# Loading 112 rows of keys instead of 128, and taking a norm's root one part later in VectorE's order, in a fused attention and feed-forward kernel

## The chip, the cores and the metric

The kernel runs on one core of one Trainium2 chip. The metric is the device time of one execution in microseconds, as the median of several runs. TensorE (PE in the profile) does the matmuls, VectorE (DVE) and GpSimd (POOL) elementwise work, ScalarE (ACT) activations and copies, and SyncE (SP) issues nearly all DMA transfers.

## The reference

Eight batches of 576 tokens, eight heads of 64 columns: a linear attention without softmax, a root-mean-square norm per token and head, and a feed-forward layer with an exact gelu over all 4608 tokens (512 to 2048 to 512), all in float32.

```python
def _attn_ref(q, k, v, g_norm):
    kv = np.einsum('bhsd,bhse->bhde', k, v)
    out = np.einsum('bhsd,bhde->bhse', q, kv)
    rms = np.sqrt(np.mean(out * out, axis=-1, keepdims=True) + 1e-06)
    return (out / rms * g_norm).astype(np.float32)

def _moe_ref(x, w_in, w_out):
    h = x @ w_in
    g = 0.5 * h * (1.0 + erf(h * np.float32(1.0 / np.sqrt(2.0))))
    return (g @ w_out).astype(np.float32)
```

## The kernel before

The 4608 tokens are cut into nine chunks of 512. Every instruction's place is set by the order in which the code is written, engine by engine; there is no scheduler that reorders.

**Keys and values.** For each batch `b` and pair of heads `p`, the sum of keys times values (`sum_kv`, matmuls on line 175) needs 576 rows: four blocks of 112 rows side by side in one tile (`kv_main`, 4 KB per row) and a tail of 128 rows. In memory the 112 rows of `kv_main` are padded with zeros to 128. `load_kv` (the transfer on line 130) brings all 128 rows, and the matmuls use the first `KROWS` = 112. The sums lie in a bank of PSUM called `a0` or `a1`, and `place_kv` copies them out (line 186 on ScalarE, line 188 twice on VectorE). All four pairs of batch 0 and of batch 1 are loaded at the start, eight of the 32 loads, among the activations `qT` and the weights, all on SP's one queue.

**The start.** Twelve warm-up matmuls (line 782) run on TensorE while the first loads land. Then come, for chunk 0: the key sums of batch 0, pair by pair, the projections (line 229), the squares (ScalarE), the root (VectorE, lines 299 to 305), and in between the key sums of pairs 0 and 1 of batch 1. Line 894 expands the root over the heads on TensorE, lines 885 and 900 multiply it in on VectorE, and line 660 is the first matmul of the feed-forward layer. Weights are split into high and low halves on ScalarE and VectorE as they arrive.

**Chunks 2 to 8** use sums and differences of blocks of the weights, seven products where eight would be. Layer 1 is a row of parts: `first_part(j)` is 24 matmuls, `second_part(j)` 18 (line 559), for j from 0 to 7, in the order first 0, first 1, second 0, first 2, second 1, first 3, second 2, first 4, second 3 and so on. Part j uses one of three pairs of PSUM banks, chosen by `j % 3`, so first part 5 takes the banks acc2 and acc3 of part 2 again. What frees those banks are the two gelus of second part 2 (line 591, ScalarE), and ahead of each gelu stand sums on VectorE (line 550):

```python
    def second_part(at, j, blocks):
        ...
        add(a[:, right], a[:, right], u[:, right])
        product(at, j, 6, b[:, right])
        add(v[:, left], b[:, right], u[:, left])
        add(b, b, v)
```

While chunk c runs, the next chunk's norm is prepared between the parts (`within_layer1`). For chunk 2 (`FAST`), the squares are summed after first part 3 (`fold`), the key sums of pairs 0 and 1 of batch 4 follow on TensorE, and then the root: `rsqrt` issues nine small VectorE instructions (lines 296 to 314), `place_kv` one copy on ScalarE and two on VectorE. The root is spread by VectorE (line 327) and multiplied in by GpSimd (line 323) from second part 2 on (`SCALES`). In `within_layer1` a place is written `(j, second)`: `(3, False)` is behind first part 3, `(2, True)` behind second part 2, which comes next.

Of the kernel before, what the change touches and what calls it, by code (L numbers as in the profile page):

```python
# [19 lines left out]
KROWS = 112  # L20
# [3 lines left out]
FAST = 2  # L24
# [13 lines left out]
def linear_attn_rms_gelu_ffn(  # L38
# [16 lines left out]
    nc = tc.nc  # L55
# [19 lines left out]
    def bank(name):  # L75
        return psum.tile([P, 512], F32, name=name)
# [27 lines left out]
    def block_tile(name, dtype):  # L104
        return const.tile([P, 2 * DM + EXTRA.get(name, 0)], dtype, name=name)
# [7 lines left out]
    def late_tile(name):  # L113

        if name not in late:
            late[name] = block_tile(name, I32)[:, :2 * DM].bitcast(F32)
        return late[name]

    def load_kv(b, p):

        early = b == 0 or (b == 1 and p > 1)
        if early:
            main = late_tile(f"w_out{NF - 1 - p if b == 0 else NF - 3 - p}")
        elif b == 2 and p > 1:
            main = block_tile(f"s{p - 1}", F32)
        elif b > 2 and b != FAST + 2 and p > 1:
            names["keys", p], main = take(stays=True)
        else:
            main = work.tile([P, 2 * DM], I32, name="kv_main", bufs=2).bitcast(F32)
        nc.sync.dma_start(out=main, in_=kv_main[b, p])  # L130
        main = main.rearrange("p (a n) -> p a n", a=2)[:KROWS]
        if b == 0:
            tails = late_tile(f"w_in{NF - 1}")[:TAIL].rearrange("p (a n) -> p a n", a=NP)
            if p == 0:
                nc.sync.dma_start(out=tails, in_=kv_tail[0])
            tail = tails[:, p]
        else:
            at = slice((p - 2) * 2 * P, (p - 1) * 2 * P)
            if early:
                tail = late_tile(f"w_in{NF - 5}")[:, at]  # L140
            elif b == 2 and p > 1:
                if p == 2:
                    kv_ps["tails"] = block_tile("s0", F32)
                tail = kv_ps["tails"][:, at]
            elif b > 2 and b != FAST + 2 and p > 1:
                if p == 2:
                    names["keys", 0], kv_ps["tails"] = take(stays=True)
                tail = kv_ps["tails"][:, at]
            else:
                tail = work.tile([P, 2 * P], I32, name="kv_tail", bufs=2).bitcast(F32)  # L150
            tail = tail[:TAIL]
            nc.sync.dma_start(out=tail, in_=kv_tail[b, :, p])
        tail = tail.rearrange("p (a n) -> p a n", a=2)
        parts = [main[:, :, j * P:(j + 1) * P] for j in range(NJ)] + [tail]
        kv_in[b, p] = [(t[:, 0], t[:, 1]) for t in parts]
# [6 lines left out]
    def rows(r):  # L162
        return slice(r * D, (r + 1) * D)

    def sum_kv(b, pairs, ps=None, first=0):

        if ps is None:
            first = pairs[0]
            ps = kv_ps[b, first] = next_bank("a")
        for p in pairs:  # L170
            n = p - first
            for j, (k, v) in enumerate(kv_in.pop((b, p))):

                for r in (slice(0, D), slice(D, 2 * D)):
                    nc.tensor.matmul(  # L175
                        out=ps[r, n * D:(n + 1) * D], lhsT=k[:, r], rhs=v[:, r],
                        start=(j == 0), stop=(j == NJ),
                    )

    def place_kv(b, pairs):  # L180

        ps = kv_ps.pop((b, pairs[0]))
        ps = ps[:, :len(pairs) * D].rearrange("p (n d) -> p n d", d=D)
        at = slice(pairs[0], pairs[-1] + 1)
        t = kv[b % 2]
        nc.scalar.copy(out=t[:, at, 0], in_=ps)
        for r in range(2):
            nc.vector.tensor_copy(out=t[rows(r), at, 1], in_=ps[rows(1 - r)])
# [346 lines left out]
    def take(dtype=F32, stays=False, first=()):  # L535
        name = next(n for n in [*(n for n in first if n in free), *free]
                    if not (stays and n in RINGS))
        free.remove(name)
        return name, block_tile(name, dtype)[:, :2 * DM]
# [211 lines left out]
    g_row = late_tile(f"w_in{NF - 6}")[:1, P:2 * P]  # L751
    ones, eps = (late_tile(f"w_in{NF - 6}")[:1, a * P:(a + 1) * P] for a in (2, 3))
    load_kv(0, 0)
    first.load(0)
    load_kv(0, 1)
    first.load(1)
    for p in (2, 3):
        load_kv(0, p)
# [34 lines left out]
    for d in range(0, 2 * D, BLK):  # L793
        h = d // D * D
        nc.gpsimd.tensor_tensor(
            out=fold[:, d:d + BLK], in0=ident[:, h:h + BLK], in1=ident[:, h + BLK:h + 2 * BLK],
# [24 lines left out]
    def column(n, t):  # L821
        return n_fold + 2 * ((n - 2) * NG + t)

    def sum_squares(n):
# [12 lines left out]
        out=half_g, in0=ps[:, :1], scalar1=0.5, scalar2=None, op0=ALU.mult  # L837
# [3 lines left out]
        out=sums[:, :P], lhsT=ones, rhs=eps, start=True, stop=False,  # L841
# [4 lines left out]
        out=root_g, in0=half_g, scalar1=D ** 0.5, scalar2=None, op0=ALU.mult  # L846
# [9 lines left out]
    for half in range(2):  # L856
# [6 lines left out]
        out=sums[:, :n_fold].rearrange("p (g b) -> p g b", g=2), lhsT=fold,  # L863
# [3 lines left out]
    for half in range(2):  # L867
        nc.scalar.activation(
            out=first.block((1, half)),
            in_=first.ps.pop((1, half)).rearrange("p (a n) -> p a n", a=2), func=AF.Copy,  # L870
# [11 lines left out]
    for half in range(2):  # L882
# [3 lines left out]
            out=first.o_all[:, half], in0=first.ps.pop((0, half)), scalar=root_g, in1=bc,  # L886
# [4 lines left out]
        for t in range(NG):  # L891
            for h in range(2):
                at = column(n, t) + h
                nc.tensor.matmul(
                    out=bc[rows(h), t * P:(t + 1) * P],
# [210 lines left out]
    for s in range(PLAIN * NF):  # L1106
        c, i = divmod(s, NF)
# [182 lines left out]
    def scale_next(c, at):  # L1290

        nxt = attn[c + 1]
        for n, (when, block) in enumerate(SCALES[c]):
            if when == at:
                if n % 2 == 0:
                    names["spread"], spreads[:] = zip(*(take() for _ in range(2)))
                nxt.scale(block, nc.gpsimd, spreads[n % 2][:, :CH])
                if n % 2:
                    free.extend(names.pop("spread"))
        for k in ADDS[c].get(at, ()):  # L1300
            nxt.add_blocks(k, nc.gpsimd)

    def within_layer1(c, j, second):

        at = j, second
        if c + 1 < NCH:
            nxt = attn[c + 1]
            if c == FAST and j == 0:
                if second:
                    nxt.project(1, [bank(f"a{half}") for half in range(2)])  # L1310
                for half in range(2):
                    nxt.squares((int(second), half))
            if c == FAST and at == (3, False):
                sums[c] = nxt.fold(bank("a0"))
                kv_ps[c + 2, 0] = bank("a1")
                sum_kv(c + 2, (0, 1), kv_ps[c + 2, 0])
            if at == ((3, False) if c == FAST else (0, False)):
                nxt.inv = nxt.rsqrt(sums.pop(c))
                if c + 2 < B:
                    place_kv(c + 2, (0, 1) if c == FAST else range(NP))  # L1320
            scale_next(c, at)
        if c == FAST and second and j in (2, 3):
            load_kv(c + 2, j)
        if c == FAST + 1 and at == (0, True):
            attn[c + 2].load(1)
# [49 lines left out]
    for c in range(FAST, NCH):  # L1375
        at = attn[c]
# [3 lines left out]
        for j, second in parts_of_layer1():  # L1380
# [16 lines left out]
            if j < NJ2 - 1:  # L1397
                within_layer1(c, j, second)
# [73 lines left out]
```

## Time and profile before

| | |
|---|---|
| median of three runs | 775.45 us (775.06 to 775.83) |
| profiled execution | 776.38 us, of which its span (first to last instruction) 774.6 us |
| TensorE matmuls | 768.6 us busy, 99% of the span |
| VectorE | 582.7 us, 75% |
| ScalarE | 358.4 us, 46% |
| GpSimd | 180.5 us, 23% |
| DMA queue of SP | 243.83 MB, 87.4% of 16 engines |
| granted TensorE clock | 1.0 throughout |

In the rows of a timeline the columns are the start and the duration in us, the engine (PEld is TensorE's weight load, SPq the issue of a transfer), the line, the operation, the tiles and their shape; brackets hold the idle time ahead of it and what ended that. In a list of waits they are the engine and line, what was waited for, the total in us, how often, and the longest. In a row by window stand the window, the busy times of PE, PEld, DVE, ACT and POOL, the clock, the DMA share and GB/s.

### The profile page before, as it was taken

To read this page: it belongs to the slowest core of one execution; us is meant where nothing else is said; L and a number is where in the kernel's file an instruction comes from. 1 tells how busy PE (TensorE), PEld (TensorE's weight loads), DVE (VectorE), ACT (ScalarE), POOL (GpSimd) and SP (SyncE) were. 2 spreads that over 40 slices of the span, in tenths; PEclk is the share of its full clock that TensorE was granted. 3 is DMA by queue.
4 is the path that set the end of the run, shared out by engine and by line. 5 is a ranking of instruction groups with operands and counts; after the bars stand their busy time and mean duration, and the time that the engine had idled before them with its cause. 6 is when DMAs were issued, how large, how long until landed. Compare 5 with 4: busy or idle time off the path is not lost.

```text
span 774.6 us, 16805 instructions
## 1 busy us (share of the span) xinstructions
PE 768.6 (99%) x6604; PEld 727.1 (94%) x6604; DVE 582.7 (75%) x1043; ACT 358.4 (46%) x689; POOL 180.5 (23%) x155
## 2 busy tenths in 40 slices
PE   8999999999999999999999999999999999999998
PEld 7888888888899999999999999999999999999998
DVE  3999867989878994679577857686778776955784
ACT  3777635533464571347135633454245524632460
POOL 1000025433736200620054004500450045001200
PEclk9999999999999999999999999999999999999999
DMA  9999953869999999979998899879996899799974
GB/s 345 407 409 357 369 191 132 290 231 337 331 370 370 318 340 347 365 268 327 403 336 296 320 402 333 317 222 336 380 336 215 299 355 337 245 316 346 333 246 167
DMA packets 90177, 244.89 MB, mean 316 GB/s; under 512 B 8948, under 2 KB 31988, under 8 KB 90100
## 3 DMA queue, kind: packets, MB, share of 16 engines
q1 hardware_dynamic: 90096, 243.83, 87.4%
q8 instruction: 52, 0.85, 0.4%
q14 instruction: 25, 0.20, 0.1%
q10 hardware_dynamic: 4, 0.00, 0.0%
HBM read 207.09 MB, written 34.08 MB: 311 GB/s over the span
## 4 chain that ended last, share of the span: by engine, by line
PE 94%; DMA 2%; DVE 2%; ACT 1%; issue 0%; SPq 0%; ACTq 0%
PE acc L1233 24%; PE acc L559 20%; PE h L559 12%; PE acc L693 11%; PE h L670 11%; PE h L1233 6%; PE a L1233 5%; PE a L175 2%; DMA kv_main<-kv_main 1%; PE a L229 1%; PE h L660 1%; DMA w_in<-qT 1%; PE acc L229 1%; DVE w_out L1017 0%; PE a L281 0%
## 5 line engine op out<-in xcount | busy, mean ns | idle before, releaser
L693 PE MATMUL acc<-w_out,gh 128*128 128x512 f32 x256 | 79.3, 391 | 0.0
L670 PE MATMUL h<-x,w_in 128*128 128x512 f32 x264 | 70.5, 391 | 0.0
L559 PE MATMUL acc<-w_in,w_in 128*128 128x256 f32 x510 | 66.3, 277 | 0.6 <-ACT x L591 0.6
L1233 PE MATMUL acc<-w_in,w_in 128*128 128x256 f32 x528 | 65.0, 276 | 0.0
L559 PE MATMUL acc<-x,w_in 128*128 128x256 f32 x480 | 64.0, 276 | 0.0
L559 PEld LDWEIGHTS acc<-w_in,w_in 128*128 128x128 f32 x510 | 61.7, 188 | 1.3 <-ACT x L591 0.8
L1233 PEld LDWEIGHTS acc<-w_in,w_in 128*128 128x128 f32 x528 | 62.2, 188 | 0.0
L670 PEld LDWEIGHTS h<-x,w_in 128*128 128x128 f32 x264 | 49.2, 188 | 10.7 <-ACT w_in L646 0.3
L559 PEld LDWEIGHTS acc<-x,w_in 128*128 128x128 f32 x480 | 58.9, 188 | 0.0
L693 PEld LDWEIGHTS acc<-w_out,gh 128*128 128x128 f32 x256 | 47.7, 188 | 10.1 <-issue 0.2
L693 PE MATMUL acc<-w_out,gl 128*128 128x512 f32 x128 | 49.8, 389 | 0.0
L550 DVE TENSOR_TENSOR gl<-acc,gh 128x256 f32<-128x256 f32 (+1 forms) x77 | 34.2, 444 | 20.3 <-ACT gh L572 16.4
L679 ACT ACTIVATE gh<-h 128x512 fp32r<-128x512 f32 x32 | 19.1, 598 | 60.5 <-PE h L670 60.5
L559 PE MATMUL h<-w_in,w_in 128*128 128x256 f32 x306 | 40.1, 278 | 0.0
L559 PE MATMUL h<-x,w_in 128*128 128x256 f32 x288 | 39.0, 278 | 0.0
L572 ACT COPY gh<-h 128x256 f32<-128x256 f32 x21 | 7.8, 372 | 67.3 <-PE h L559 67.3
L1233 PE MATMUL acc<-w_in,w_out 128*128 128x256 f32 x306 | 38.9, 276 | 0.0
L323 POOL TENSOR_TENSOR o<-o,w_in 128x512 f32<-128x512 f32 x10 | 13.0, 1298 | 107.9 <-ACT s L591 54.2
L550 DVE TENSOR_TENSOR gl<-h,gh 128x256 f32<-128x256 f32 x42 | 17.6, 419 | 26.2 <-ACT gh L572 23.5
L559 PEld LDWEIGHTS h<-w_in,w_in 128*128 128x128 f32 x306 | 37.2, 188 | 0.1
L1233 PEld LDWEIGHTS acc<-w_in,w_out 128*128 128x128 f32 x306 | 36.6, 188 | 0.0
L559 PEld LDWEIGHTS h<-x,w_in 128*128 128x128 f32 x288 | 35.5, 188 | 0.0
(374 smaller groups left out, 1906.3 us busy)
## 6 DMA issues: line engine op xcount, KB each, us to landing
w_in<-products_in SPq DMA_DIRECT2D x168, 512.0 KB, 5.5
w_in<-products_out SPq DMA_DIRECT2D x133, 512.0 KB, 5.0
products_in<-w_in SPq DMA_DIRECT2D x36, 256.0 KB, 5.4
w_in<-w_in SPq DMA_DIRECT2D x16, 512.0 KB, 10.2
kv_main<-kv_main SPq DMA_DIRECT2D x16, 512.0 KB, 5.7
w_out<-w_out SPq DMA_DIRECT2D x16, 512.0 KB, 10.2
q<-qT SPq DMA_DIRECT2D x15, 512.0 KB, 6.7
products_out<-w_out SPq DMA_DIRECT2D x16, 256.0 KB, 6.4
```

The source lines that it names most:

```text
L175: nc.tensor.matmul(out=ps[r, n * D:(n + 1) * D], lhsT=k[:, r], rhs=v[:, r], start=(j == 0), stop=(j == NJ),)
L229: nc.tensor.matmul(out=ps[rows(h), p % 2 * HALF + a:p % 2 * HALF + e], lhsT=kv[b % 2][rows(half), p, h ^ half], rhs=q[rows(half), h, a:e], ...
L323: eng.tensor_tensor(out=o, in0=o, in1=bc, op=ALU.mult)
L550: return eng.tensor_tensor(out=out, in0=x, in1=y, op=op)
L559: nc.tensor.matmul(out=out, lhsT=y, rhs=x[:, z, kb], start=first and kb + i == 0, stop=kb == 1 and i == 2, skip_group_check=True,)
L572: nc.scalar.copy(out=u[:, left], in_=a[:, left])
L660: nc.tensor.matmul(out=h[:, half * HALF:(half + 1) * HALF], lhsT=ws[i].bitcast(F32)[:, p * P:(p + 1) * P], rhs=at.block((p // 2, half))[:, ...
L670: nc.tensor.matmul(out=h, lhsT=parts["in", i][:, w][:, p * P:(p + 1) * P], rhs=at.x[p][:, x], start=(m + p == 0), stop=(m == 2 and p == NP ...
L679: nc.scalar.activation(out=gh, in_=h, func=AF.Gelu)
L693: nc.tensor.matmul(out=ps, lhsT=x[:, ts], rhs=parts["out", i][:, w], start=(i == 0 and m == 0), stop=(m == 2 and (i == NF - 1 or (i, t) == ...
L1233: nc.tensor.matmul(out=self.bank[name][a][:, a * HALF:(a + 1) * HALF], lhsT=x[:, at], rhs=y, start=(k in (0, 2, 1) and n + p + m == 0 and ...
```

## The change

Both edits are one line each. The load takes the first 112 rows, in the tile and in memory. In chunk 2 the root and the copies of the key sums are issued behind second part 2 instead of ahead of it; `fold` and the key sums themselves stay where they are.

```diff
@@ -127,7 +127,7 @@
             names["keys", p], main = take(stays=True)
         else:
             main = work.tile([P, 2 * DM], I32, name="kv_main", bufs=2).bitcast(F32)
-        nc.sync.dma_start(out=main, in_=kv_main[b, p])
+        nc.sync.dma_start(out=main[:KROWS], in_=kv_main[b, p, :KROWS])
         main = main.rearrange("p (a n) -> p a n", a=2)[:KROWS]
         if b == 0:
             tails = late_tile(f"w_in{NF - 1}")[:TAIL].rearrange("p (a n) -> p a n", a=NP)
@@ -1314,7 +1314,7 @@
                 sums[c] = nxt.fold(bank("a0"))
                 kv_ps[c + 2, 0] = bank("a1")
                 sum_kv(c + 2, (0, 1), kv_ps[c + 2, 0])
-            if at == ((3, False) if c == FAST else (0, False)):
+            if at == ((2, True) if c == FAST else (0, False)):
                 nxt.inv = nxt.rsqrt(sums.pop(c))
                 if c + 2 < B:
                     place_kv(c + 2, (0, 1) if c == FAST else range(NP))
```

VectorE's order in chunk 2 before, from the last sum of first part 3 on (m, y and t are the root's, a_2658 the key sums, acc_2553 and acc_2554 the banks of part 2):

```order
L550 TENSOR_TENSOR gh<-h_2624,gh 128x256
L296 TENSOR_SCALAR m<-a_2656 128x64
L299 TENSOR_SCALAR y<-m 128x64
L305 SCALAR_TENSOR_TENSOR t<-y 128x64
L310 TENSOR_TENSOR t<-t,m 128x64
L305 SCALAR_TENSOR_TENSOR t<-t 128x64
L305 SCALAR_TENSOR_TENSOR y<-t,y 128x64
L305 SCALAR_TENSOR_TENSOR t<-y 128x64
L314 TENSOR_TENSOR t<-t,m 128x64
L305 SCALAR_TENSOR_TENSOR y<-t,y 128x64
L188 COPY kv_68<-a_2658 64x2x64 x2
L550 TENSOR_TENSOR acc_2553<-acc_2553,gh 128x256
```

The same place after:

```order
L550 TENSOR_TENSOR gh<-h_2624,gh 128x256
L550 TENSOR_TENSOR acc_2553<-acc_2553,gh 128x256
L550 TENSOR_TENSOR gl<-acc_2554,gh 128x256
L550 TENSOR_TENSOR acc_2554<-acc_2554,gl 128x512
L296 TENSOR_SCALAR m<-a_2656 128x64
L299 TENSOR_SCALAR y<-m 128x64
L305 SCALAR_TENSOR_TENSOR t<-y 128x64
L310 TENSOR_TENSOR t<-t,m 128x64
L305 SCALAR_TENSOR_TENSOR t<-t 128x64
```

The three sums of second part 2 now stand ahead of the root's nine instructions and the two copies instead of behind them; the spread of the root (L327) follows next in both.

ScalarE's order there before, from the copy of first part 3's first product on:

```order
L572 COPY gh<-h_2623 128x256
L186 COPY kv_68<-a_2658 128x2x64
L591 ACTIVATE x_2716<-acc_2553 128x2x256
L591 ACTIVATE w_in_2717<-acc_2554 128x2x256
L572 COPY gh<-acc_2728 128x256
```

And after:

```order
L572 COPY gh<-h_2623 128x256
L591 ACTIVATE x_2701<-acc_2553 128x2x256
L591 ACTIVATE w_in_2702<-acc_2554 128x2x256
L186 COPY kv_68<-a_2658 128x2x64
L572 COPY gh<-acc_2728 128x256
```

The copy of the key sums goes behind the two gelus of part 2. TensorE's order is unchanged, and on SP only the shape of the key loads differs. The first of them, after:

```order
L130 DMA w_out_118<-kv_main 112x1024
L135 DMA w_in_120<-kv_tail 128x1024
L203 DMA w_in_122<-qT 128x512
L130 DMA w_out_124<-kv_main 112x1024
L203 DMA w_in_122<-qT 128x512
L130 DMA w_out_127<-kv_main 112x1024
L130 DMA w_out_129<-kv_main 112x1024
L203 DMA w_in_131<-qT 128x512 x2
L611 DMA w_in_136<-w_in 128x1024
L130 DMA kv_main<-kv_main 112x1024
L152 DMA kv_tail<-kv_tail 128x256
L130 DMA kv_main<-kv_main 112x1024
```

Every row of `kv_main` read 128x1024 before; no transfer has moved past another.

## The prediction

> **What bounds the kernel now.** I read the page first (busy time by engine, the chain that ended last), then what TensorE's matmuls (PE) waited for, then the timeline round the two places that the change touches.
>
> ```profile
> PE 768.6 (99%) x6604; PEld 727.1 (94%) x6604; DVE 582.7 (75%) x1043; ACT 358.4 (46%) x689; POOL 180.5 (23%) x155
> ...
> q1 hardware_dynamic: 90096, 243.83, 87.4%
> ...
> PE 94%; DMA 2%; DVE 2%; ACT 1%; issue 0%; SPq 0%; ACTq 0%
> ```
>
> ```profile
> PE acc L559 <- ACT x L591: 0.6, 1, 0.6
> ...
> PE a L175 <- DMA kv_main<-kv_main: 0.4, 1, 0.4
> ```
>
> PE is busy for 768.6 of 774.6 us. The chain is PE's for 94%, so an edit pays only where PE stands still or is held back. From 29 us to the end the list of PE's waits holds a single entry, 0.6 us for a gelu (L591) in chunk 2; before that, one wait for a load of keys, 0.4 us. The change touches just these two. The DMA engines are at 87% in the mean, but PE waits for no transfer after that one, so the key loads after the start, however long, are put at nothing: their cover is that they are issued several parts ahead. The profiled execution took 776.38 us, 0.93 us above the median of the runs (775.45). I subtract the same microseconds from both.
>
> **Part 1, the root in chunk 2.** The timeline of that place, by engine rather than by time:
>
> ```profile
> 230.58 0.84 PE L559 MATMUL acc<-x,w_out 128*128 128x256 f32 x6
> ...
> 233.98 0.84 PE L559 MATMUL h<-w_in,w_in 128*128 128x256 f32 x6
> ...
> 236.76 3.67 PE L559 MATMUL acc<-w_in,w_in 128*128 128x256 f32 x30 [0.58 <-ACT x L591]
> ...
> 241.63 2.88 PE L559 MATMUL h<-w_in,w_in 128*128 128x256 f32 x24
> ...
> 232.08 0.41 DVE L550 TENSOR_TENSOR gh<-h,gh 128x256 f32<-128x256 f32 x1
> 232.41 0.21 DVE L296 TENSOR_SCALAR m<-a 128x64 f32<-128x64 f32 x1
> ...
> 234.91 0.23 DVE L305 SCALAR_TENSOR_TENSOR y<-t,y 128x64 f32<-128x64 f32 x1
> 235.15 0.59 DVE L188 COPY kv<-a 64x128 f32<-64x128 f32 x2
> 235.66 0.41 DVE L550 TENSOR_TENSOR acc<-acc,gh 128x256 f32<-128x256 f32 x1
> ...
> 236.57 0.70 DVE L550 TENSOR_TENSOR acc<-acc,gl 128x512 f32<-128x512 f32 x1
> 237.18 0.70 DVE L327 STREAM_TRANSPOSE s<-y 128x512 f32<-128x512 f32 x1
> 238.20 0.42 DVE L550 TENSOR_TENSOR gl<-acc,gh 128x256 f32<-128x256 f32 x1 [0.32 <-ACT gh L572]
> ...
> 236.11 0.60 ACT L591 ACTIVATE x<-acc 128x512 f32<-128x512 f32 x1 [5.37 <-DVE acc L550]
> ```
>
> The six matmuls at 230.58 are the last of second part 2, so both its banks are complete at 231.42. VectorE (DVE) gets to their sums only at 235.66: from 232.41 it runs the root's nine instructions and the two copies of a key sum, 235.66 - 232.41 = 3.25 us. The gelu that frees bank acc2 starts at 236.11, and PE, which is to put first part 5 into that bank, stands until 236.76.
>
> What PE loses: a first part is 24 matmuls, a second part 18. Second part 3 starts at 233.98; it (18), first part 5 (24) and second part 4 (18) follow, then first part 6 at 241.63. Second part 4 ends where first part 6 begins, so 60 matmuls took 7.65 us. The undisturbed pace comes from two rows, 24 matmuls in 2.88 us and 6 in 0.84: (2.88 - 0.84) / 18 = 0.1133 each, so 60 take 6.80. The loss is 0.85 us, of which the named wait is 0.58, the rest the refill round it. I take 0.85, since both ends of that count are starts of matmuls in the trace.
>
> What takes its place: with the sums first, the three run from 232.41 for the 1.52 us that they take now (235.66 to 237.18), to 233.93. The first gelu follows 0.45 us behind the first sum (as 236.11 behind 235.66), the second at 233.95, and with 0.60 each both banks are free by 234.6; PE wants them at 233.98 + 18 x 0.1133 = 236.02. Then come the nine root instructions and two copies, 3.25 us: they end at 237.18, where the first spread of the root (L327) starts now, so it is no later. On ScalarE (ACT) the copy of the key sum goes behind two gelus; its reader is a projection in the second layer, several parts on. GpSimd (POOL) waits for the spreads and so gets them at the same time or earlier: the 0.32 wait at 238.20 goes too, because the ScalarE copy it waited for was itself queued behind the late gelus. SP's queue and its order are unmoved here. So nothing on the moved path becomes later; the nine instructions cost nothing while VectorE's sums stay ahead of PE.
>
> What is late next: the gelu for first part 7.
>
> ```profile
> 245.11 0.60 ACT L591 ACTIVATE x<-acc 128x512 f32<-128x512 f32 x1 [2.75 <-DVE acc L550]
> ...
> 246.39 2.88 PE L559 MATMUL acc<-w_in,w_in 128*128 128x256 f32 x24
> ```
>
> It ends at 245.71, 0.68 us ahead of the matmuls that need its bank. PE comes 0.85 us earlier, so VectorE's chain must come at least 0.17 earlier; the vanished 0.32 us wait covers that. If it did not, 0.17 and a refill (0.85 - 0.58 = 0.27) would be lost again. Part 1: **-0.85 us**, bounds -0.4 and -0.85.
>
> **Part 2, 112 rows instead of 128.** Each load of keys shrinks from 512 to 448 KB. Eight of them stand among the first loads, where the queue is always full:
>
> ```profile
> 6.50:21.30 14.80, 13.55 (x214) 10.68 (x213) 8.34 (x26) 5.32 (x12) 0.00 (x0) 1.00 1.03 401
> 21.30:29.70 8.40, 8.40 (x75) 7.23 (x73) 8.26 (x15) 6.25 (x11) 0.00 (x0) 1.00 1.03 405
> ```
>
> The last two columns are the DMA engines' share (1.03) and GB/s (401): a load of 524288 bytes takes 1.31 us of a full queue, one of 448 KB 1.14. That is 0.16 us per load if the time goes with the bytes, nothing if it goes with something else. The landings, two views side by side (the issues, and the time from issue to landing, of the second, fourth and sixth load):
>
> ```profile
> 2.12 0.43 SPq L130 DMA_DIRECT2D w_out<-kv_main  x1
> ...
> 4.58 0.33 SPq L130 DMA_DIRECT2D w_out<-kv_main  x1
> ...
> 9.11 0.33 SPq L130 DMA_DIRECT2D kv_main<-kv_main  x1
> ```
>
> ```profile
> w_out<-kv_main SPq DMA_DIRECT2D x1, 512.0 KB, 6.3
> ...
> w_out<-kv_main SPq DMA_DIRECT2D x1, 512.0 KB, 7.1
> ...
> kv_main<-kv_main SPq DMA_DIRECT2D x1, 512.0 KB, 9.6
> ```
>
> Second load in at 8.42, fourth at 11.68, sixth at about 18.75. Their users:
>
> ```profile
> 6.47 0.60 PEld L175 LDWEIGHTS a<-w_out 112*64 112x64 f32 x16 [0.23 <-issue]
> ...
> 8.73 0.37 PEld L175 LDWEIGHTS a<-w_out 112*64 112x64 f32 x10 [0.39 <-issue]
> ...
> 10.93 0.55 PEld L175 LDWEIGHTS a<-w_out 112*64 112x64 f32 x16 [0.39 <-issue]
> ...
> 11.76 0.58 PEld L175 LDWEIGHTS a<-w_out 112*64 112x64 f32 x16 [0.17 <-PE a L175]
> ...
> 17.86 0.30 PEld L782 LDWEIGHTS h<-w_in 128*128 128x128 f32 x2
> 18.79 0.55 PEld L175 LDWEIGHTS a<-kv_main 112*64 112x64 f32 x16 [0.63 <-DMA kv_main<-kv_main]
> ...
> 19.43 1.92 PE L894 MATMUL acc<-w_in,y 128*64 128x128 f32 x32
> ...
> 18.43 0.21 DVE L305 SCALAR_TENSOR_TENSOR y<-t,y 128x48 f32<-128x48 f32 x1
> ...
> 20.59 0.69 DVE L900 TENSOR_TENSOR o<-o,acc 128x512 f32<-128x512 f32 x1 [0.41 <-PE acc L894]
> ```
>
> At 18.79 the sixth load is the gate: the weight loads sat idle 0.63 us after 18.16. After the same warm-up matmuls (L782) they sat 0.23 at 6.47, so 0.40 of it is the load's. It goes if the sixth load comes 0.40 earlier: six loads at 0.16 give 0.98, more than enough. At 11.76 the fourth load, in at 11.68, holds PE by up to 0.17; four loads at 0.16 give 0.65, and some 0.15 goes. That 0.15 travels, because copies, projection, squares and root follow one another there. At 8.73 PE starts 0.31 after the landing, but the same 0.39 of idle stands before 10.93, so I take it for PE's own change of shape and count nothing. The first load is covered by the warm-up.
>
> What is next: the expansion of the root over the heads (L894) can't start before the root is there, 18.64. It starts at 19.43, so up to 0.79 is open and 0.40 + 0.15 passes. VectorE then waits 0.41 for L894's first half (20.59) and from there is busy for 8.26 of 8.40 us; it shifts by the same 0.41 plus the 0.15. So weights and activations are split earlier by as much as PE comes earlier, and PE, without a wait from 29 us on, carries it to the end. The bounds of part 2 are 0 (loads no shorter) and 0.94 (18.79 back to 18.16, which is 0.63, 0.15 for the fourth load, and 0.39 - 0.23 = 0.16 for the second); I take 0.50, nearest to the idle rows at 18.79 and 11.76.
>
> One rule speaks against it. The Trainium skill, "SBUF — State Buffer", section "Door 1: The DMA port swizzle", says that a transfer's rate hangs on the 16 ports that its partitions reach, eight partitions to a port; by its formula rows 0 to 111 leave eight rows on twelve ports and four on the other four. Where ports set the pace, 112 rows would then take as long as 128; part 2 would be 0 by it, against the 0.50 above, and no row of this trace shows a load of fewer rows.
>
> **The sum.** 0.85 + 0.50 = 1.35 us: 776.38 becomes 775.03 for a profiled execution, and 775.45 becomes **774.1** for the median. That is 0.17%; about 0.2% (1.55 us) is what a measurement of this kernel can tell from no change.
>
> **The rivals.**
> - The start gives all it can, because the second load too gates PE (8.42, then 8.73) and the idle after the warm-up vanishes whole: 0.94 + 0.85 = 1.8 us, 773.7. For it: the landing lies close ahead of 8.73. Against: the equal 0.39 at 10.93. Chance 0.25.
> - The loads land no earlier, since the slowest of the parallel paths still carries eight rows: 0.85 us remains, 774.6. For it: 401 GB/s at a share of 1.03 says that something is saturated, not what. Against: nothing in the rows. Chance 0.14; the port rule above is its reason.
> - Part 1 pays less: the gelu for first part 7 does not come forward, PE waits there, 0.4 us goes back: 0.95 us, 774.5. Chance 0.10.
> - The move does nothing, because the sums at 235.66 wait for something other than the root's turn: 0.50 us, 774.95. Against: their banks are complete at 231.42 and VectorE is never idle between. Chance 0.04.
> - Slower: 112 rows are dealt to fewer DMA engines than 16, and each load takes longer by d. The sixth load then comes 6d late and holds PE at 18.79 for it, against the 0.85 won later. It is slower than before from d = 0.14 us on, and by 1.55 us from d = 0.40, a load of 1.71 us, as on twelve engines (1.31 x 16/12 = 1.75: 6 x 0.44 - 0.85 = +1.8, 777.2). On eight engines the load is 2.62 and the sum +7.0. Chance 0.05. The Trainium skill, "DMA: Bandwidth & Descriptors", section "Why a DMA increments its semaphore by 16 and not by 1", says the largest number up to 16 that divides the rows is used, which is 16 for 112; no run here shows it yet.
>
> **How the numbers follow.** The forecast has the remaining 0.42. Faster by over 0.2% is the first rival, 0.25, and 0.08 of the forecast's upper edge (measured medians spread by some 0.4 us: 775.06 to 775.83): 0.33. Slower is 0.05. Within 0.2% is the rest, 0.62. The range goes from the first rival with that spread, 773.3, to the emptiest cases of the same sign, 775.5; it leaves out the slower case and some of the edges, under 2 in 10.
>
> **What would show it.** In the profile after: no wait of L559 for L591 near 236 us, the three sums ahead of L296, 60 matmuls from second part 3 to first part 6 in about 6.8 us, and the gelu for first part 7 ending ahead of its matmuls. At the start: the sixth key load landing before 18.2, the weight loads after the warm-up idle by about 0.2 instead of 0.63, L894 near 18.9. If L894 stays near 19.4, part 2 is wrong; if a new wait stands at first part 7 or in layer 2, part 1 is; if key loads take over 1.4 us each, the slower rival holds.

## The result and the profile after

The changed kernel takes 782.55 us (779.18 to 784.22, six runs), the kernel before 775.64 us beside it (775.06 to 777.32, six runs). The ratio is 1.0073, with a 95% interval from 1.0053 to 1.0092: it is slower by 0.7%, where 774.1 us had been forecast. The medians differ by 6.9 us, and the interval of the ratio is 4.1 to 7.1 us. The profiled execution of after took 784.22 us, its span 782.4 us, against 776.38 and 774.6 before.

The page of after first: busy time, the queue of SyncE (packets, MB, share of 16 engines), and the chain that ended last.

```profile
PE 771.3 (99%) x6604; PEld 728.8 (93%) x6604; DVE 582.4 (74%) x1043; ACT 358.2 (46%) x689; POOL 180.1 (23%) x155
...
q1 hardware_dynamic: 89584, 241.73, 89.1%
...
PE 90%; DMA 5%; DVE 3%; ACT 1%; issue 1%; SPq 0%; ACTq 0%; DVEq 0%
```

The line to stop at is the queue's. It moves 2.10 MB less than before (241.73 against 243.83) and yet keeps the engines busy for longer, 89.1% of a longer span against 87.4%. The chain, which was 94% PE and 2% DMA, is now 90% and 5%.

What PE's matmuls waited for in after (total us, times, longest):

```profile
PE acc L1233 <- DMA w_in<-products_out: 2.8, 3, 2.1
PE a L175 <- DMA w_out<-kv_main: 1.3, 3, 0.7
PE acc L559 <- ACT x L591: 1.1, 1, 1.1
...
PE acc L559 <- DVE gl L550: 0.6, 1, 0.6
```

Before, L559 stood in this list once, with 0.6 us, and the second layer (L1233) not at all. Now there are three new places: the key sums at the start (L175), chunk 2 (L559), and the second layer, where PE waits for fetches of weight products.

**Chunk 2.** The timeline of after at the place of the moved root:

```profile
233.72 0.60 ACT L591 ACTIVATE x<-acc 128x512 f32<-128x512 f32 x1 [2.28 <-DVE acc L550]
...
234.65 0.21 DVE L296 TENSOR_SCALAR m<-a 128x64 f32<-128x64 f32 x1
...
235.16 0.84 PE L559 MATMUL h<-w_in,w_in 128*128 128x256 f32 x6
...
237.08 0.42 SPq L130 DMA_DIRECT2D kv_main<-kv_main  x1
...
241.96 2.88 PE L559 MATMUL h<-w_in,w_in 128*128 128x256 f32 x24
...
245.43 0.92 PE L559 MATMUL acc<-w_in,w_in 128*128 128x256 f32 x6 [0.58 <-DVE gl L550]
...
248.80 3.06 PE L559 MATMUL acc<-w_in,w_in 128*128 128x256 f32 x24 [1.09 <-ACT x L591]
```

Up to 241.96 this is what part 1 described: the gelu of part 2 starts ahead of the root (L296), the wait for it has gone, and the 60 matmuls from second part 3 (235.16) to first part 6 (241.96) take 6.80 us instead of 7.65. Then two waits follow that the kernel before does not have. The first is put down to a sum on VectorE, but that name is inferred. By the trace's transfer records a fetch of products issued at 236.71, just ahead of the key load at 237.08, landed at 245.29, 0.14 us ahead of the matmuls at 245.43; the same fetch before was issued at 235.53 and landed at 241.40, with second part 5 at 244.35. The second wait is for the gelu of the part delayed by the first. Between 241.96 and 248.80 after falls back by 2.1 us against before, more than the 0.85 won.

**The rates.** Busy times by window (PE, PEld, DVE, ACT, POOL), the clock, the DMA share and GB/s. Before:

```profile
8.00:13.00 5.00, 4.63 (x84) 3.10 (x84) 1.42 (x8) 1.64 (x5) 0.00 (x0) 1.00 1.04 408
236.00:250.00 14.00, 13.42 (x118) 13.24 (x117) 11.23 (x23) 6.26 (x14) 10.72 (x9) 1.00 1.00 381
355.00:380.00 25.00, 25.00 (x281) 24.81 (x279) 18.14 (x30) 13.48 (x25) 0.00 (x0) 1.00 1.01 388
```

After, with the stretch 6.5 to 21.3 that the prediction shows of before:

```profile
6.50:21.30 14.80, 12.41 (x195) 9.71 (x192) 7.63 (x24) 4.89 (x12) 0.00 (x0) 1.00 1.04 329
8.00:13.00 5.00, 3.33 (x59) 2.11 (x55) 1.00 (x5) 1.51 (x4) 0.00 (x0) 1.00 1.04 306
236.00:250.00 14.00, 12.33 (x107) 11.99 (x106) 11.40 (x26) 4.63 (x9) 10.73 (x9) 1.00 1.03 321
355.00:380.00 25.00, 22.93 (x194) 22.76 (x193) 19.40 (x32) 13.47 (x25) 0.00 (x0) 0.96 1.02 332
```

The DMA share is full in every row, and the rate falls by 14 to 25%: 401 to 329, 408 to 306, 381 to 321, 388 to 332 GB/s. In 32 to 50 us, where no key load is in the queue, the kernels move 408 and 407 GB/s. So in these stretches, in which key loads are under way, the engines are as busy as before and move less.

**The start.** The weight loads after the landings, and L894:

```profile
11.39 0.55 PEld L175 LDWEIGHTS a<-w_out 112*64 112x64 f32 x16 [0.71 <-DMA w_out<-kv_main]
...
12.82 0.58 PEld L175 LDWEIGHTS a<-w_out 112*64 112x64 f32 x16 [0.77 <-PE a L175]
...
19.70 0.55 PEld L175 LDWEIGHTS a<-kv_main 112*64 112x64 f32 x16 [0.48 <-DMA kv_main<-kv_main]
...
20.33 1.92 PE L894 MATMUL acc<-w_in,y 128*64 128x128 f32 x32
```

The same three groups of weight loads stood at 10.93, 11.76 and 18.79, and L894 at 19.43. The fourth key load lands at 12.71 instead of 11.65, the sixth at 19.66 instead of 18.75.

**The second layer.** The place of the longest new wait, PE's timeline, first before (without a wait), then after:

```profile
371.74 2.88 PE L1233 MATMUL acc<-w_in,w_in 128*128 128x256 f32 x24
```

```profile
373.80 1.41 PE L1233 MATMUL acc<-w_in,w_in 128*128 128x256 f32 x11
377.28 2.44 PE L1233 MATMUL acc<-w_in,w_in 128*128 128x256 f32 x12 [2.07 <-DMA w_in<-products_out]
```

The wait is not all that is lost here. From 377.8 to 381.2 us the granted clock is 0.50, and the matmuls come 0.21 us apart instead of 0.11: 12 of them take 2.44 us where they took 1.52. Of the 3.9 us that after loses between 371 and 378 of before, about 2.2 are the wait and 1.6 the slow clock behind it.

Compare the start of each matmul in after with the start of the same matmul in before, at its time in before. PE in after is behind by 0.1 us at 8.7, 1.1 at 12, 0.9 at 18.8, 1.1 just before the moved root takes effect, 0.3 just after (236.98), 2.4 at 246, 1.9 at 337 (before itself ran slowly there), 5.9 at 378 and 7.8 at 456. After that it stays. So the 7.8 us of this profile come from the start, chunk 2 and the second layers of chunks 2 and 3.

### The profile page after: what moved, and what is told of

It is laid out like the page before. It is cut to its first block, busy times and chain, and to the rows that moved or that the text cites. A ratio compares the mean times of both kernels' runs of the same rounds, so it can differ in the third digit from the quotient of the medians.

```text
span 782.4 us, 16804 instructions
## 1 busy us (share of the span) xinstructions
PE 771.3 (99%) x6604; PEld 728.8 (93%) x6604; DVE 582.4 (74%) x1043; ACT 358.2 (46%) x689; POOL 180.1 (23%) x155
## 3 DMA queue, kind: packets, MB, share of 16 engines
q1 hardware_dynamic: 89584, 241.73, 89.1%
## 4 chain that ended last, share of the span: by engine, by line
PE 90%; DMA 5%; DVE 3%; ACT 1%; issue 1%; SPq 0%; ACTq 0%; DVEq 0%
PE acc L1233 22%; PE acc L559 19%; PE h L559 12%; PE acc L693 11%; PE h L670 11%; PE h L1233 6%; PE a L1233 5%; DMA w_in<-products_out 3%; PE a L175 2%; DMA kv_main<-kv_main 1%; PE a L229 1%; DMA w_in<-qT 1%; PE h L660 1%; PE acc L229 1%; DVE w_out L1017 0%
## 5 line engine op out<-in xcount | busy, mean ns | idle before, releaser
L1233 PE MATMUL acc<-w_in,w_in 128*128 128x256 f32 x528 | 66.5, 279 | 2.4 <-DMA w_in<-products_out 2.3
L559 PE MATMUL acc<-w_in,w_in 128*128 128x256 f32 x510 | 66.3, 277 | 1.7 <-ACT x L591 1.1
L1233 PEld LDWEIGHTS acc<-w_in,w_in 128*128 128x128 f32 x528 | 63.2, 190 | 2.9 <-issue 2.6
L559 PEld LDWEIGHTS acc<-w_in,w_in 128*128 128x128 f32 x510 | 61.7, 188 | 2.5 <-ACT x L591 1.3
L559 PE MATMUL acc<-x,w_in 128*128 128x256 f32 x480 | 63.8, 276 | 0.0
L559 PEld LDWEIGHTS acc<-x,w_in 128*128 128x128 f32 x480 | 58.7, 188 | 0.0
L559 PE MATMUL h<-w_in,w_in 128*128 128x256 f32 x306 | 40.2, 278 | 0.0
L1233 PE MATMUL acc<-w_in,w_out 128*128 128x256 f32 x306 | 39.0, 276 | 0.0
L559 PE MATMUL h<-x,w_in 128*128 128x256 f32 x288 | 38.8, 277 | 0.0
L559 PEld LDWEIGHTS h<-w_in,w_in 128*128 128x128 f32 x306 | 37.3, 188 | 0.2
L1233 PEld LDWEIGHTS acc<-w_in,w_out 128*128 128x128 f32 x306 | 36.7, 188 | 0.1
L559 PEld LDWEIGHTS h<-x,w_in 128*128 128x128 f32 x288 | 35.4, 188 | 0.0
```

The source lines that it names most:

```text
L559: nc.tensor.matmul(out=out, lhsT=y, rhs=x[:, z, kb], start=first and kb + i == 0, stop=kb == 1 and i == 2, skip_group_check=True,)
L1233: nc.tensor.matmul(out=self.bank[name][a][:, a * HALF:(a + 1) * HALF], lhsT=x[:, at], rhs=y, start=(k in (0, 2, 1) and n + p + m == 0 and ...
```

## The experiments

All kernels below are edits of the kernel before. The runs of before beside them took 775.57 us (20 runs; first four experiments), 775.86 us (19 runs; the next three) and 775.78 us (13 runs; the last two). The theory: loads of 112 rows occupy the DMA engines for longer, not shorter, and slow what stands behind them. The rivals: the moved root costs the time, only the start suffers, or the number of bytes or transfers does it.

### The root alone

```diff
-            if at == ((3, False) if c == FAST else (0, False)):
+            if at == ((2, True) if c == FAST else (0, False)):
```

> Only the root is moved; loads keep 128 rows. Theory A (the loss is the loads' alone): no wait of L559 near 236 us, 60 matmuls from second part 3 to first part 6 in 6.8 us, no new wait in second part 5 or first part 7, and the time 0.85 us under before, about 774.7. Theory B (the moved root makes the waits that the changed kernel has at second part 5 and first part 7, 0.6 and 1.1 us): these waits stand here too and the time is 0.5 to 1 us over before.

Measured: 774.51 us, 1.1 us below the median of before, ratio 0.9986 (0.9976 to 0.9996). All of PE's waits in its profile:

```profile
PE h L782 <- DVE w_in L749: 1.1, 1, 1.1
PE h L828 <- ACT gl L817: 0.4, 1, 0.4
PE acc L229 <- ACT kv L186: 0.3, 1, 0.3
PE a L175 <- DMA w_out<-kv_main: 0.2, 1, 0.2
```

No wait of L559 and none in the second layer, as theory A expected. Against before, PE gains 0.85 us by 236.98 (60 matmuls in 6.80 us) and gives 0.26 back at first part 7, so 0.6 net in this profile. The move makes the kernel faster by itself, and the loss of after does not come with it alone.

### The 112 rows alone

```diff
-        nc.sync.dma_start(out=main, in_=kv_main[b, p])
+        nc.sync.dma_start(out=main[:KROWS], in_=kv_main[b, p, :KROWS])
```

> Only the loads take 112 rows; the root stays where it was. Theory A: the whole loss and the part that the root gave back, 6 to 8 us over before (the change's 6.9 plus 0.85, less what overlaps), with a start 0.9 us later at L894 and about 306 GB/s from 8 to 13 us where before has 408. Theory B: one to two microseconds less loss than the change, and no waits at second part 5 and first part 7.

Measured: 780.82 us, ratio 1.0063 (1.0041 to 1.0085). Its rates and its waits:

```profile
8.00:13.00 5.00, 2.90 (x53) 2.10 (x55) 0.89 (x4) 1.51 (x4) 0.00 (x0) 1.00 1.04 299
...
236.00:250.00 14.00, 13.62 (x116) 13.43 (x116) 11.93 (x28) 5.28 (x11) 9.38 (x7) 1.00 1.03 334
```

```profile
PE a L175 <- DMA w_out<-kv_main: 1.8, 3, 0.9
PE acc L1233 <- DMA w_in<-products_out: 1.7, 5, 0.5
```

The loss is 1.7 us less than the change's in the medians, as theory B expected; the 6 to 8 us of theory A are not reached. The rates and two of the three places of after are there without the moved root. The third is not: in 236 to 250 the fetch that after waits for lands at 244.78, but here PE keeps its old wait for the gelu and comes later. In after the faster PE runs into the late fetch, and the root's gain goes there. Whether the root even costs time together with the short loads is not settled: after lies 1.7 us above this kernel in the medians, but their runs overlap (779.18 to 784.22 and 777.91 to 782.80).

### 112 rows at the start only, and after the start only

```diff
-        nc.sync.dma_start(out=main, in_=kv_main[b, p])
+        n = KROWS if b < 2 else P
+        nc.sync.dma_start(out=main[:n], in_=kv_main[b, p, :n])
```

> 112 rows for the first eight key loads alone (batches 0 and 1), 128 for the other 24; root as before. If the start's late landings are one part of the loss and the later loads, which delay the fetches of weight products, the rest: +0.9 us over before, the shift of L894, and no waits for transfers in the second layer. If a late start shifts everything against the fetches and so makes the later waits as well: +4 us or more.

Measured: 777.54 us, ratio 1.0026 (1.0016 to 1.0036), no wait for a fetch in the second layer. That is +2.0 us, twice the 0.9 expected and half of the 4. Its rate, and a wait that before does not have:

```profile
8.00:13.00 5.00, 3.89 (x76) 2.83 (x76) 0.93 (x5) 1.73 (x5) 0.00 (x0) 1.00 1.04 335
```

```profile
PE a L176 <- DMA kv_tail<-kv_tail: 0.6, 1, 0.6
```

In this profile the sixth key load lands at 17.79, earlier than in before, and PE stands for the tail that follows it on the queue. L894 starts at 19.86. Over all profiles it starts at 19.86 to 20.33 in the three with 112 rows at the start, and at 18.70 to 19.43 in the three with whole loads there (before, the root alone, and the next experiment). So the start is later with 112 rows, but which transfer PE waits for, and by how much, changes from one execution to the next; this profile does not place the whole 2.0 us. The opposite edit (`n = P if b < 2 else KROWS`):

> 128 rows for the eight key loads of batches 0 and 1, 112 for the 24 later ones; the root as before. Theory A (a load of 112 rows slows whatever shares the queue with it, also later, where fetches of weight products stand behind it): what 112 rows cost in all, less what they cost at the start, +4.96 - 1.97 = about +3 us (778.5 to 779.5); the start as before (about 405 GB/s in 8 to 13 us), and waits of layer 2 for a fetch of products_out, 1.5 us or more in all. Rival B (only the start suffers, and the later loads are hidden): within 0.5 us of before.

Measured: 777.75 us, ratio 1.0027 (1.0016 to 1.0039). Its rate at the start is whole. Of its waits (lines are one higher here), the one for key loads (L176) stands at the start, where the loads are whole. The rate, then the waits:

```profile
8.00:13.00 5.00, 4.00 (x78) 2.83 (x76) 0.98 (x5) 1.63 (x5) 0.00 (x0) 1.00 1.04 409
```

```profile
PE acc L1234 <- DMA w_in<-products_out: 0.8, 2, 0.4
PE a L176 <- DMA w_out<-kv_main: 0.7, 2, 0.5
```

Its PE falls back against before by 1.3 us between 369 and 375 us and by 0.8 at 455 to 457, in the two second layers. So the eight loads at the start cost 2.0 us and the 24 others 2.0 us as well: "only the start suffers" falls, but the later loads cost less than the 3 us that I expected. The two together are 4.0 us, inside the interval of the 112 rows alone (0.41 to 0.85%, 3.2 to 6.6 us). The waits listed were half of what I expected too, since a late fetch also shows as matmuls that start singly.

The parts do not add up to the change. In ratios, the root alone (-0.14%), the start (+0.26%) and the later loads (+0.27%) make 0.39%; after has 0.73%. The difference, 0.34% or some 2.6 us, is a little beyond what the intervals allow, so it seems that something is lost only when all three act together. The profile of after shows two such places, the late fetch that meets the faster PE in chunk 2 and the halved clock behind the wait of 2.07 us. No experiment takes them apart.

### 120 rows, and 96 rows

```diff
-        nc.sync.dma_start(out=main, in_=kv_main[b, p])
+        nc.sync.dma_start(out=main[:120], in_=kv_main[b, p, :120])
```

> Loads of 120 rows, root as before; nothing is left out. Theory 'uneven shares' (112 rows are dealt as sixteen shares of seven, which no longer lie one to a path; 120 would be fifteen shares of eight): the stream from 8 to 13 us stays near 400 GB/s or loses a sixteenth, and the time is within 1 us of before. Theory 'any count but 128 is slow': about 310 to 350 GB/s there and 3 us or more over before.

Measured: 792.89 us, ratio 1.0217 (1.0200 to 1.0233).

```profile
8.00:13.00 5.00, 2.81 (x44) 1.67 (x38) 0.57 (x3) 1.30 (x3) 0.00 (x0) 0.96 1.04 254
18.00:24.00 6.00, 5.30 (x31) 5.05 (x29) 2.31 (x8) 2.79 (x5) 0.00 (x0) 0.50 1.03 285
```

254 GB/s, below what either theory expected, and in the second row a granted clock of 0.50, after PE had stood at the start. The 17 us are therefore not the loads' alone. The edit to 96 rows (the same with `:96`, the matmuls too):

> Loads of 96 rows (six to a share), root as before; rows 96 to 111 of each block of keys and values are left out of the sums. A quarter of the bytes of each key load is gone. If bytes set the time of a load: 0.33 us less per load, L894 0.4 to 0.6 us earlier, time 0.4 us under before. If the sharing of paths does: packets stay long (under 350 GB/s from 8 to 13 us), the load takes 1.2 to 1.4 us in spite of a quarter fewer bytes, and the time is from level to 4 us over before.

Measured: 780.34 us, ratio 1.0065 (1.0041 to 1.0089), 305 GB/s in 8 to 13 us, much as the theory of shared paths expected. A quarter of the bytes less than 128 rows, and the kernel is still slower: the time does not go with the bytes.

### Fewer bytes in all 128 rows

```diff
-        nc.sync.dma_start(out=main, in_=kv_main[b, p])
+        nc.sync.dma_start(out=main[:, :896], in_=kv_main[b, p, :, :896])
```

> 128 rows of 3584 bytes instead of 4096: the same 448 KB as the changed kernel, but all rows; root as before. The last block's values are left out (the block before stands in for them). If the rows' number is what hurts: about 400 GB/s from 8 to 13 us, the sixth load landing 0.6 to 1 us earlier, L894 0.4 to 0.55 earlier and the time 0.4 to 0.55 us under before, as the prediction's second part had it. If smaller loads as such are slow: a loss of 3 us or more as with 112 rows.

The bytes of 112 rows, in another shape. Measured: 775.67 us, ratio 0.9997 (0.9986 to 1.0008), so no difference that can be told. The rate is whole:

```profile
8.00:13.00 5.00, 4.69 (x85) 3.33 (x87) 1.66 (x9) 1.64 (x5) 0.00 (x0) 1.00 1.04 411
```

so smaller loads as such are not slow. The sixth key load lands at 17.67 instead of 18.75, with its sums at 18.27 instead of 18.79. That looks like the half microsecond that part 2 meant to buy, but it is not shown to be: with the root alone, where the loads are the same as in before, the sixth lands at 17.81 and its sums start at 18.07. The sums of this kernel, then of the root alone:

```profile
18.27 0.55 PEld L176 LDWEIGHTS a<-kv_main 112*64 112x64 f32 x16
```

```profile
18.07 0.55 PEld L175 LDWEIGHTS a<-kv_main 112*64 112x64 f32 x16
```

Executions with the same loads differ there by more than the half microsecond, and the medians can't tell it apart either.

### Halves and stripes

Every load as two transfers of 64 rows, with all its bytes; first rows 0 to 63 and 64 to 127:

```diff
-        nc.sync.dma_start(out=main, in_=kv_main[b, p])
+        for n in range(2):
+            half = slice(n * 64, (n + 1) * 64)
+            nc.sync.dma_start(out=main[half], in_=kv_main[b, p, half])
```

> Each key load as two transfers, rows 0 to 63 and 64 to 127; all bytes as before, root as before. If what counts is which rows are written at the same time, each half uses half of the paths: packets about twice as long while a half runs (250 to 320 ns instead of 159), 300 to 350 GB/s from 8 to 13 us, and 4 us or more over before. If it is only an odd share (seven rows) that hurts: near 400 GB/s, and within 1 us of before, apart from 32 more issues of 0.33 us on SP.

Measured: 804.35 us, ratio 1.0349 (1.0299 to 1.0398). The rate is far below the 300 to 350 GB/s of the first theory.

```profile
8.00:13.00 5.00, 2.91 (x20) 1.77 (x22) 0.76 (x4) 0.21 (x1) 0.00 (x0) 0.59 1.07 211
```

Then the even rows and the odd rows (`main[n::2]`, `kv_main[b, p, n::2]`):

> Each key load as two transfers of 64 rows, the even rows and then the odd rows, all bytes; the root as before. Theory A (the pace hangs on how many of the 16 ports a transfer reaches at a time): even or odd rows alone reach all 16, so the rate at the start is clearly above the 211 GB/s that two halves of consecutive rows gave, 254 to 400, and the time is at most half of their excess, below 790. Rival B (any transfer of 64 rows is slow, or a second transfer per load is what costs): about 211 GB/s and +28 us, as with consecutive halves.

Measured: 779.34 us, ratio 1.0040 (1.0025 to 1.0055).

```profile
3.00:8.00 5.00, 4.18 (x38) 3.86 (x38) 0.00 (x0) 0.01 (x1) 1.45 (x7) 1.00 0.95 303
8.00:13.00 5.00, 4.70 (x43) 2.92 (x44) 1.21 (x6) 0.73 (x3) 0.00 (x0) 0.61 1.04 402
```

The same bytes in the same number of transfers of the same number of rows: 402 GB/s with the rows spread over the tile, 211 with them packed into half of it. That rules out the number of rows and the number of transfers as the cause of the lost rate. Of what stripes cost, 3.6 us, PE has lost 2.3 by 18.8 us in the profile: the first row still shows 303 GB/s at a share of 0.95, and the second a granted clock of 0.61. SyncE issues twice as many transfers there (the third at 3.10 us, where before issued its second load at 2.12); that this is what delays the start is likely, but not tested.

### The packets

The trace also records each packet. Durations of those of 3.5 to 4 KB between 8 and 13 us, key loads and others together, in ns (10th percentile, median, 90th), beside the rate of that stretch and the time against before:

| key loads | packets, ns | GB/s | time, us |
|---|---|---|---|
| 128 rows | 159, 159, 161 | 408 | 0 |
| 128 rows of 3.5 KB | 140, 140, 167 | 411 | -0.2 |
| 2 x 64, stripes | 159, 159, 159 | 402 | +3.6 |
| 112 rows (after) | 172, 229, 271 | 306 | +6.9 |
| 96 rows | 166, 256, 274 | 305 | +4.5 |
| 120 rows | 221, 268, 316 | 254 | +17.3 |
| 2 x 64, halves | 262, 309, 387 | 211 | +28.5 |

The packets themselves become longer, in the 112-row kernel nine of ten above 172 ns, though other transfers of 128 rows share the stretch. The neighbours can be seen apart from the key loads: all packets of 2 KB there belong to the activations `qT`, four loads of 128 rows that no edit touches. Their median is 84 ns with whole key loads, with loads of 3.5 KB per row and with stripes, and 100 with 112 rows, 93 with 96, 127 with 120 and 168 with halves. So the short loads slow their neighbours as well. Which rows a transfer holds decides it: the three kernels whose transfers reach evenly over all 128 rows have short packets, the four that leave out a block at the end, or fill one half, have long ones. One rival is left open: each edit picks the same rows in the tile and in memory, so no run tells whether the slow side is the writing of the tile or the reading of memory.

The Trainium skill, "SBUF — State Buffer", section "Door 1: The DMA port swizzle", says that a transfer's rate hangs on how many of 16 ports its partitions reach, that partitions 0 to 63 reach eight of them, and that 128 reach all. By its formula the even rows reach all 16 too. Halves at 211 and stripes at 402 GB/s agree with it. It does not give the sizes for the rest: with eight rows on the busiest port, as with 128 rows, 112 rows by themselves would run at 408 x 112/128 = 357 GB/s and 120 at 382, both estimates from that page's formula, while 306 and 254 were measured in a stretch that other transfers share. So the port count alone does not give these rates, and why 120 rows are worse than 96 is open.

## Why the prediction was wrong

**The step that failed first** is the size of a load in part 2: "a load of 524288 bytes takes 1.31 us of a full queue, one of 448 KB 1.14", or 1.31 at worst. Both ends took a row's rate as the queue's property and asked only how many bytes go through it. The trace of before showed 401 GB/s at a share of 1.03, and a share of 1.03 says that the engines are busy, not that they would be as fast for other shapes. With 112 rows the queue runs at 299 to 335 GB/s from 8 to 13 us, in three profiles; in after the sixth load lands 0.91 us later instead of 0.98 earlier, which is 0.15 us more per load over six. The term was +2.0 us at the start (the experiment with 112 rows there only), where -0.50 with bounds of 0 and -0.94 stood. An end on the side of a loss was owed here, as no row showed a load of fewer rows.

The gain was mis-sized too. The 0.63 us of idle at 18.79, of which part 2 wanted 0.40, belongs to that one execution of before: with the same loads it is 0.17 with 112 rows after the start only, and not there at all with the root alone. So even loads that shrink as hoped need not have paid 0.50.

**The second step that failed** is the sentence that puts the key loads after the start at nothing, "however long", because they are issued several parts ahead. The list of waits does show no wait for them, and in after PE still does not wait for one of them after the start. It waits for the fetches of products that stand on the same queue behind them: 2.0 us for these loads with the root left where it was. The cover was right for the loads and was never worked out for what they delay.

**The rule** of the ports was weighed, and its result taken as "part 2 would be 0 by it". It was the one place in the prediction that asked which rows a load reaches, but it was applied to the load alone and not to the packets beside it, and gave a chance of 0.14 to no gain and none to a loss.

**The slower rival** had the place (the sixth load at 18.79) and the quantity (d per load), and the point from which it decides (0.14 us) lies near the 0.15 of after. That nearness is luck: against the other two profiles with whole loads at the start (17.81 and 18.33) the same landing gives 0.31 and 0.22 us per load. Its cause, fewer than 16 engines, is not what happened. A load counts 16 increments of its semaphore. With 112 rows all of them come late, the first 3.35 us after the issue (3.17 with 128 rows); with 120 rows one comes at 0.58 us and the other fifteen from 3.8 us on, as where one engine has no part. By the rule that the prediction cites from the Trainium skill, "DMA: Bandwidth & Descriptors", section "Why a DMA increments its semaphore by 16 and not by 1", 112 rows are dealt to 16 engines; the increments agree. And it was priced at the start alone: by its sum, six times 0.15 less 0.85 would have been +0.1 us, of the 6.9 measured.

**Part 1** was right in its mechanism: no wait near 236, the three sums ahead of L296, 60 matmuls in 6.80 us, GpSimd and VectorE not later. Alone it measures 1.1 us in the medians (0.3 to 1.9 by the interval), and 0.60 in one profile, where the forecast was 0.85 with bounds of 0.4 and 0.85. The 0.26 lost at first part 7, 0.18 of it ahead of the first matmul, is the loss of 0.17 and a refill that part 1 named under "What is late next" and held to be covered; it was not. In after the 0.85 is won at 236 and lost at 245 to the late fetch.

**The signs.** The prediction named three things that would make it wrong: L894 staying near 19.4, "a new wait stands at first part 7 or in layer 2", and "key loads take over 1.4 us each". L894 came at 20.33, the waits came, and the loads, by the landing in after, took 1.31 and 0.15 more, 1.46 us. The waits were put down to part 1 there; the experiments give those in the second layer to the short loads, and the two in chunk 2 to the late fetch and the faster PE together.

## What to carry to other kernels

Before a transfer is cut to the rows that are used, ask which rows stay: 128 full rows of a padded tile were faster than 112 of them, and the same saving of bytes taken from the length of each row did no harm, though no gain was measured either. Before a wait is priced from one profile, see in a second execution of the same kernel, or of one with the same code there, whether it stands there too. A busy share of 100% tells how long the engines work and not what they move; read GB/s beside it, stretch by stretch. Where a transfer is "covered", work out the cover for everything that stands behind it on the queue.

Of the versions here, the moved root with loads of 128 rows has the lowest median: 774.51 us, 0.9986 of before and 8.0 us below the median of after.

## What else the runs showed

- One shape of load slows its neighbours: packets of `qT`, which did not change, went from 84 to 100 ns (median) beside key loads of 112 rows and to 168 beside halves.
- A pause of PE can cost twice. With 120 rows the granted clock was 0.50 in 18 to 24 us, with halves 0.59 and with stripes 0.61 in 8 to 13 us, where before had 1.00. In after it was 0.50 for 3.4 us behind a wait of 2.07 us, far from the start.
- Executions of the same loads differ at the start: with the root alone PE was 0.73 us ahead of before at 18.8, though nothing there differs. Five of the eleven profiles also have a stretch of 18 to 34 us in which PE runs about 4% slower (before at 318 to 336, the root alone at 704 to 732), each at another place; no experiment shows why. One profile tells no less than about 1 us.
